# Linear attention beside dilated attention: W2 = KV Wo from 32x32 array tiles, KV^T from 32-column tiles

## The chip, the cores and the metric

The kernel runs on one core of a Trainium2 chip. The time is the device time of one launch in microseconds. Before the change it is 491.19 us, the median of three runs (490.68 to 491.39); the profiled execution has a span of 489.7 us.

## The reference: two attention blocks on one input, mixed by a gate

```python
# x: 2048 x 1024 bf16; 32 heads of 32
g = sigmoid((x * gate_w).sum(-1, keepdims=True))
out = g * A(x) + (1 - g) * B(x)

def A(x):                                   # linear attention
    q, k, v = split_heads(x @ wqkv_A)
    phi = lambda t: where(t > 0, t + 1, exp(t)) + 1e-6
    pq, pk = phi(q), phi(k)
    kv  = einsum("bhsd,bhse->bhde", pk, v)  # one 32x32 matrix per head
    z   = einsum("bhsd->bhd", pk)
    num = einsum("bhqd,bhde->bhqe", pq, kv)
    den = einsum("bhqd,bhd->bhq", pq, z)[..., None] + 1e-6
    return merge_heads(num / den) @ wo_A

def B(x):                                   # window of 8 keys, 2 apart, softmax
    ...
    return merge_heads(o) @ wo_B
```

## The kernel before

Block A is rearranged. With KV a block-diagonal matrix of 32 blocks of 32x32, one per head, the output is (pq / den) (KV Wo), so the kernel folds KV into Wo once and calls the product W2; W2 overwrites Wo in SBUF. KV itself comes from G = x^T pk, as KV^T = pk^T V = G^T Wv, of which only the diagonal blocks are wanted. The ratio g / (1 - g) = exp(x . gate_w) is folded into the normalised pq, and the evacuation of the last product scales with 1 - g.

The order of stages is: phi(K) of A, G, KV^T, V of B (with the W2 products set between its matmuls), Q of A beside the rest of V, then K and Q of B with the scores and their products with V set between, and last the two output products in one accumulation. TensorE's instructions keep the order in which the code gives them.

The loads at the start are issued in this order, all from SyncE's queue but one:

```python
WkA = [wpool.tile([P, KT, 512], BF16, name="WkA0", tag="wa")]
nc.sync.dma_start_transpose(out=xT[:, :, 0:P], in_=rows(x, 0, P))
for i in range(4):
    if i == 2:
        nc.sync.dma_start_transpose(out=xT[:, :, P:2 * P], in_=rows(x, P, 2 * P))
    (nc.sync if i else nc.scalar).dma_start(            # the first quarter: ScalarE's queue
        out=WkA[0][:, 2 * i:2 * i + 2, :], in_=A_wqkv[...])
for t in range(2, NB):                                  # 14 more transposes
    nc.sync.dma_start_transpose(out=xT[:, :, t * P:(t + 1) * P], in_=rows(x, t * P, (t + 1) * P))
WkA += load_w("WkA", A_wqkv, D, "wa", only=(1,))        # the second half of Wk
...
```

TensorE runs 36 small products of ones first, and then phi(K) for row blocks 0 and 1 in the order in which the quarters come: depths 0 to 3 of block 0, depths 0 to 3 of block 1, then 4 and 5 of both, then 6 and 7 of both. KV^T and W2:

```python
for c in range(KT):                    # eight chunks of 128 columns, four heads in each
    kvp = ps_1.tile([P, P], F32, name="kv_ps", tag="p1")
    for kt in range(KT):
        nc.tensor.matmul(kvp[:], lhsT=WvA[c // 4][:, kt, (c % 4) * P:(c % 4 + 1) * P],
                         rhs=G[c // 4][:, kt, (c % 4) * P:(c % 4 + 1) * P],
                         start=(kt == 0), stop=(kt == KT - 1))
    nc.vector.tensor_tensor(out=KVT[:, c, :], in0=kvp[:], in1=bdmask[:], op=ALU.mult)
...
def w2_event(c):
    def go():
        for half in range(2):
            w2p = bank1()              # one of six banks of ps_1
            nc.tensor.matmul(w2p[:], lhsT=KVT[:, c, :], rhs=WoA[half][:, c, :], start=True, stop=True)
            if half:
                nc.scalar.copy(out=WoA[half][:, c, :], in_=w2p[:])
            else:
                nc.vector.tensor_copy(out=WoA[half][:, c, :], in_=w2p[:])
    return go
...
units = [u for t in range(4) for u in v_units(t)]      # 64 V matmuls of B, groups of 8
interleave(units, [(4 + 8 * c, w2_event(c)) for c in range(KT)])
for t in range(12):
    for u in v_units(4 + t): u()
    for u in qa_units(t, bank1, qa_finish): u()
```

bdmask is 1 in the four 32x32 blocks of the diagonal and 0 elsewhere. Each Q group of A goes through phi, and each row block through the normalising, on VectorE:

```python
def phi(dst, pj):
    e = work.tile([P, 512], F32, name="e", tag="e")
    nc.scalar.activation(out=e[:], in_=pj[:], func=ACT.Exp)
    nc.vector.tensor_scalar(out=e[:], in0=e[:], scalar1=1.0, scalar2=1e-6, op0=ALU.min, op1=ALU.add)
    nc.vector.scalar_tensor_tensor(out=dst, in0=pj[:], scalar=0.0, in1=e[:], op0=ALU.max, op1=ALU.add)

def normalize(t, pq, pn, prod):
    nc.vector.tensor_tensor(out=prod, in0=pq, in1=zrow[:], op=ALU.mult)          # L274
    den = small3.tile([P, H], F32, name="den", tag="den")
    nc.vector.tensor_reduce(out=den[:], in_=prod.rearrange("p (h e) -> p h e", h=H), ...)
    nc.vector.tensor_scalar(out=den[:], in0=den[:], scalar1=1e-6, ...)           # L278
    nc.vector.reciprocal(out=den[:], in_=den[:])
    nc.vector.scalar_tensor_tensor(                                              # L280
        out=pn.rearrange("p (h e) -> p h e", h=H), in0=pq.rearrange("p (h e) -> p h e", h=H),
        scalar=ratio[:, t:t + 1], in1=den[:]..., op0=ALU.mult, op1=ALU.mult)
```

For row blocks 0 to 11 the result is written to DRAM and read back transposed; for the last four it is transposed from SBUF.

Of the kernel before, what the change touches and what calls it, by code (L numbers as in the profile page):

```python
# [9 lines left out]
ALU = mybir.AluOpType  # L10
BF16 = mybir.dt.bfloat16
F32 = mybir.dt.float32
PE = mybir.EngineType.PE
DVE = mybir.EngineType.DVE
P = 128
# [14 lines left out]
def interleave(units, events):  # L30

    events = sorted(events, key=lambda e: e[0])
    for i, unit in enumerate(units):
        while events and events[0][0] <= i:
            events.pop(0)[1]()
        unit()
    for _, fn in events:
        fn()
# [3 lines left out]
def kernel(  # L42
# [11 lines left out]
    nc = tc.nc  # L54
    S, D = A_x.shape[1:]
# [3 lines left out]
    out2 = out[0].rearrange("(m two) d -> two m d", two=2)  # L59

    def rows(ap, s0, s1):
        return ap[s0 // 1024, s0 % 1024:(s1 - 1) % 1024 + 1, :]

    H = 32
    Dh = D // H
    KT = D // P
    NB = S // P
# [4 lines left out]
    consts = ctx.enter_context(tc.tile_pool(name="consts", bufs=1))  # L72
    wpool = ctx.enter_context(tc.tile_pool(name="wpool", bufs=2))
# [5 lines left out]
    def load_w(name, src, col0, tag, only=(0, 1)):  # L79
        halves = []  # L80
        for h in only:
            w = wpool.tile([P, KT, 512], BF16, name=f"{name}{h}", tag=tag)
            c0 = col0 + h * 512
            nc.sync.dma_start(out=w[:], in_=src[:, c0:c0 + 512].rearrange("(kt p) n -> p kt n", p=P))
            halves.append(w)
        return halves
# [7 lines left out]
    WkA = [wpool.tile([P, KT, 512], BF16, name="WkA0", tag="wa")]  # L94
    nc.sync.dma_start_transpose(out=xT[:, :, 0:P], in_=rows(x, 0, P))  # L95
    for i in range(4):
        if i == 2:
            nc.sync.dma_start_transpose(out=xT[:, :, P:2 * P], in_=rows(x, P, 2 * P))
        (nc.sync if i else nc.scalar).dma_start(  # L99
            out=WkA[0][:, 2 * i:2 * i + 2, :],  # L100
            in_=A_wqkv[2 * i * P:(2 * i + 2) * P, D:D + 512].rearrange("(kt p) n -> p kt n", p=P))
    for t in range(2, NB):
        nc.sync.dma_start_transpose(out=xT[:, :, t * P:(t + 1) * P], in_=rows(x, t * P, (t + 1) * P))  # L103
    WkA += load_w("WkA", A_wqkv, D, "wa", only=(1,))
# [3 lines left out]
    WvA = load_w("WvA", A_wqkv, 2 * D, "wb")  # L108
    WoA = load_w("WoA", A_wo, 0, "wo")
# [3 lines left out]

    onesb = consts.tile([P, P], BF16, name="onesb")
    nc.vector.memset(onesb[:], 1.0)
    bdmask = consts.tile([P, P], F32, name="bdmask")
    nc.vector.memset(bdmask[:], 0.0)
    for i in range(4):
        nc.vector.memset(bdmask[32 * i:32 * i + 32, 32 * i:32 * i + 32], 1.0)


    def band(dst, lead):
# [11 lines left out]
    ratio = consts.tile([P, NB], F32, name="ratio")  # L134
    omg = consts.tile([P, NB], F32, name="omg")
    zrow = consts.tile([P, D], F32, name="zrow")
    KVT = consts.tile([P, KT, P], BF16, name="KVT")

    work = ctx.enter_context(tc.tile_pool(name="work", bufs=3))
    small3 = ctx.enter_context(tc.tile_pool(name="small3", bufs=2))  # L140
# [7 lines left out]
    with tc.manual_schedule(engines={PE}):  # L148

        with ExitStack() as s1:  # L150
            ps_1 = s1.enter_context(tc.tile_pool(name="ps_1", bufs=6, space=bass.MemoryType.PSUM))
# [37 lines left out]
            for t in range(1, NB):  # L189
                side.append(lambda t=t: nc.vector.tensor_tensor(  # L190
                    out=zacc[:], in0=zacc[:] if t > 1 else pk[:, 0, :], in1=pk[:, t, :], op=ALU.add))
            side.append(lambda: nc.gpsimd.partition_all_reduce(zrow[:], zacc[:], P, bass_isa.ReduceOp.add))
            for t in range(NB):
                side.append(lambda t=t: nc.vector.tensor_tensor_reduce(
                    out=gjunk[:], in0=xrow[:, t, :], in1=gw_row[:], scale=1.0, scalar=0.0, op0=ALU.mult,
                    op1=ALU.add, accum_out=gdot[:, t:t + 1]))

            G = []
            for half in range(2):
                g_ = kq.tile([P, KT, 512], BF16, name=f"G{half}", tag="kq")  # L200
                G.append(g_)
                for kt in range(KT):
                    pj = ps_1.tile([P, 512], F32, name="g_ps", tag="p1")
                    for t in range(NB):
                        nc.tensor.matmul(pj[:], lhsT=xrow[:, t, kt * P:(kt + 1) * P],  # L205
                                         rhs=pk[:, t, half * 512:(half + 1) * 512],
                                         start=(t == 0), stop=(t == NB - 1))
# [7 lines left out]
            nc.vector.tensor_scalar(out=omg[:], in0=ratio[:], scalar1=1.0, scalar2=None, op0=ALU.add)  # L215
            nc.vector.reciprocal(out=omg[:], in_=omg[:])

            for c in range(KT):
                kvp = ps_1.tile([P, P], F32, name="kv_ps", tag="p1")
                for kt in range(KT):  # L220
                    nc.tensor.matmul(kvp[:], lhsT=WvA[c // 4][:, kt, (c % 4) * P:(c % 4 + 1) * P],  # L221
                                     rhs=G[c // 4][:, kt, (c % 4) * P:(c % 4 + 1) * P],
                                     start=(kt == 0), stop=(kt == KT - 1))
                nc.vector.tensor_tensor(out=KVT[:, c, :], in0=kvp[:], in1=bdmask[:], op=ALU.mult)
            WkB = load_w("WkB", B_wqkv, D, "wb")


# [9 lines left out]
            def bank1():  # L237
                return ps_1.tile([P, 512], F32, name="p1_ps", tag="p1")

            def w2_event(c):  # L240
                def go():
                    for half in range(2):
                        w2p = bank1()
                        nc.tensor.matmul(w2p[:], lhsT=KVT[:, c, :], rhs=WoA[half][:, c, :], start=True, stop=True)  # L244
                        if half:
                            nc.scalar.copy(out=WoA[half][:, c, :], in_=w2p[:])
                        else:
                            nc.vector.tensor_copy(out=WoA[half][:, c, :], in_=w2p[:])
                return go

            def v_units(t):
# [21 lines left out]
# [3 lines that stand above are left out]
                nc.vector.tensor_reduce(out=den[:], in_=prod.rearrange("p (h e) -> p h e", h=H),  # L276
                                        axis=mybir.AxisListType.X, op=ALU.add)
                nc.vector.tensor_scalar(out=den[:], in0=den[:], scalar1=1e-6, scalar2=None, op0=ALU.add)  # L278
                nc.vector.reciprocal(out=den[:], in_=den[:])
                nc.vector.scalar_tensor_tensor(  # L280
                    out=pn.rearrange("p (h e) -> p h e", h=H), in0=pq.rearrange("p (h e) -> p h e", h=H),
                    scalar=ratio[:, t:t + 1], in1=den[:].rearrange("p (h o) -> p h o", o=1).broadcast_to([P, H, Dh]),
                    op0=ALU.mult, op1=ALU.mult)

            def qa_units(t, bank, evacuate):
                def mm(half, kt, st):
# [16 lines left out]
                    nc.sync.dma_start(out=pqd[t * P:(t + 1) * P, :], in_=pn)  # L303

            units = [u for t in range(4) for u in v_units(t)]
            interleave(units, [(4 + 8 * c, w2_event(c)) for c in range(KT)])
            for t in range(12):
                for u in v_units(4 + t):
                    u()
# [5 lines left out]
        with ExitStack() as s2:  # L315
# [102 lines left out]
            WoB = load_w("WoB", B_wo, 0, "wb")  # L418
            raw = wpool.tile([P, 4, D], BF16, name="raw", tag="wc")
            fw = wpool.tile([P, 2, D], F32, name="fw", tag="wc")  # L420
            pqT = [kq.tile([P, KT, 512], BF16, name="pqT0", tag="kq")]
            for t in range(4):
                nc.sync.dma_start_transpose(out=pqT[0][:, :, t * P:(t + 1) * P], in_=pqd[t * P:(t + 1) * P, :])
# [4 lines left out]
            def qa_late(t):  # L428
                r = raw[:, t - 12, :]
                for half in range(2):  # L430
                    h = slice(half * 512, (half + 1) * 512)
                    phi(r[:, h], r[:, h])
                normalize(t, r, r, fw[:, t % 2, :])
                nc.sync.dma_start_transpose(out=pqT[1][:, :, (t - 4) * P:(t - 3) * P], in_=r)

            def out_units(tb, bank):
                def mm(c0, n, side, c, st):
                    if side == 0 and c == 0:
                        st["ps"] = bank()
                    if side == 0:  # L440
                        lhsT, W = (pqT[0][:, c, tb * P:(tb + 1) * P] if tb < 4 else
                                   pqT[1][:, c, (tb - 4) * P:(tb - 3) * P]), WoA
                    else:
                        lhsT, W = OBT[:, c, tb * P:(tb + 1) * P], WoB
                    nc.tensor.matmul(st["ps"][:, 0:n], lhsT=lhsT, rhs=W[c0 // 512][:, c, c0 % 512:c0 % 512 + n],  # L445
                                     start=(side == 0 and c == 0), stop=(side == 1 and c == KT - 1))
                    if side == 0 or c < KT - 1:
                        return
                    osb = work.tile([P, 512], BF16, name="osb", tag="e")
                    nc.scalar.activation(out=osb[:, 0:n], in_=st["ps"][:, 0:n], func=ACT.Copy,  # L450
                                         scale=omg[:, tb:tb + 1])
                    (nc.sync if tb < NB - 1 else nc.scalar).dma_start(
                        out=rows(out2, tb * P, (tb + 1) * P)[:, c0:c0 + n], in_=osb[:, 0:n])
                parts = [(0, 512), (512, 512)] if tb < NB - 1 else [(0, 512), (512, 256), (768, 256)]
                for c0, n in parts:
                    st = {}
                    for side in range(2):
                        for c in range(KT):
                            yield lambda c0=c0, n=n, side=side, c=c, st=st: mm(c0, n, side, c, st)
# [51 lines left out]
```

The softmax here doesn't subtract the row's maximum and nothing guards it: scores larger than these inputs give would overflow.

## Time and profile before

| | us |
|---|---|
| median of three runs | 491.19 |
| span of the profiled execution | 489.7 |
| TensorE matmuls busy | 483.1 |
| VectorE busy | 279.1 |
| ScalarE busy | 188.0 |
| phi(K), second half of the columns, from | 35.21 |
| G from | 63.01 |
| KV^T from | 118.26 |
| V of B with W2 in between from | 121.8 |
| V of B and Q of A in turn from | 142.56 |
| K and Q of B with scores from | 221.98 |
| last stage (outputs) from | 382.75 |

A line of the profile names the source line, the engine (PE is TensorE, PEld its weight load, DVE VectorE, ACT ScalarE, SPq the queue of SyncE), the operation, and the tiles written and read. In the timeline and in the chain the first number is the start and the second the length, in microseconds; x16 is the number of instructions merged into the line; what stands in brackets is the engine's idle time before it and what ended it. [...] matmuls that follow each other every 0.22 us are shown as 0.38 us long; the rate is read from the starts.

### The profile page before, as it was taken

To read this page: it belongs to the slowest core of one execution; us is meant where nothing else is said; L and a number is where in the kernel's file an instruction comes from. 1 tells how busy PE (TensorE), PEld (TensorE's weight loads), DVE (VectorE), ACT (ScalarE), POOL (GpSimd) and SP (SyncE) were. 2 spreads that over 40 slices of the span, in tenths; PEclk is the share of its full clock that TensorE was granted. 3 is DMA by queue.
4 is the path that set the end of the run, shared out by engine and by line. 5 is a ranking of instruction groups with operands and counts; after the bars stand their busy time and mean duration, and the time that the engine had idled before them with its cause. 6 is when DMAs were issued, how large, how long until landed. Compare 5 with 4: busy or idle time off the path is not lost.

```text
span 489.7 us, 8140 instructions
## 1 busy us (share of the span) xinstructions
PE 483.1 (99%) x3332; PEld 229.5 (47%) x3332; DVE 279.1 (57%) x512; ACT 188.0 (38%) x283; POOL 16.3 (3%) x33
## 2 busy tenths in 40 slices
PE   7999999999999999999999999999999999999997
PEld 4444444446444444444454444445444444444444
DVE  1666689993329999996356666556655596000000
ACT  1333311111543333333566666666664332212121
POOL 3100001411000000000000000000000000000000
PEclk9999999999999999999999999999999999999999
DMA  9999960000521222245011151111173943111111
GB/s 195 165 289 370 348 201 0 0 1 28 194 73 59 82 95 93 72 135 174 3 38 28 32 115 30 30 36 35 31 151 82 213 87 86 33 43 33 43 34 43
DMA packets 80181, 46.56 MB, mean 95 GB/s; under 512 B 53520, under 2 KB 74128, under 8 KB 80144
## 3 DMA queue, kind: packets, MB, share of 16 engines
q1 hardware_dynamic: 79440, 45.52, 35.1%
q8 instruction: 26, 0.43, 0.4%
q10 hardware_dynamic: 704, 0.52, 0.4%
q14 instruction: 11, 0.09, 0.1%
HBM read 21.23 MB, written 7.34 MB: 58 GB/s over the span
## 4 chain that ended last, share of the span: by engine, by line
PE 92%; SPq 5%; DMA 2%; issue 0%; ACT 0%
PE kq_ps L332 23%; PE d_ps L445 21%; PE g_ps L205 11%; PE p_ps L255 11%; PE p_ps L289 8%; PE pk_ps L157 6%; SPq L103 4%; PE q_ps L289 3%; PE oB L383 3%; PE s L358 2%; DMA WkA<-in_A_wqkv_dram 2%; PE q_ps L445 1%; PE kv_ps L221 1%; PE p_ps L244 1%; SPq L99 0%; SPq L95 0%
## 5 line engine op out<-in xcount | busy, mean ns | idle before, releaser
L368 ACT ACTIVATE PT<-s 128x896 bf16<-128x896 f32 (+1 forms) x72 | 63.0, 926 | 24.5 <-PE s L358 24.5
L332 PE MATMUL kq_ps<-xT,WkB 128*128 128x512 bf16 x256 | 65.3, 379 | 0.0
L332 PE MATMUL kq_ps<-xT,WqB 128*128 128x512 bf16 x256 | 64.8, 379 | 0.0
L369 DVE TENSOR_TENSOR PT<-PT,mask 128x896 bf16<-128x896 bf16 (+1 forms) x72 | 44.6, 623 | 26.6 <-ACT PT L368 26.6
L255 PE MATMUL p_ps<-WvB,xT 128*128 128x512 bf16 x256 | 58.5, 379 | 0.0
L157 PE MATMUL pk_ps<-WkA,xT 128*128 128x512 bf16 x256 | 56.2, 379 | 2.2 <-DMA WkA<-in_A_wqkv_dram 1.6
L445 PE MATMUL d_ps<-WoA,pqT 128*128 128x512 bf16 (+1 forms) x248 | 56.9, 372 | 0.0
L445 PE MATMUL d_ps<-WoB,OBT 128*128 128x512 bf16 (+1 forms) x248 | 56.9, 372 | 0.0
L205 PE MATMUL g_ps<-pk,xrow 128*128 128x512 bf16 x256 | 55.4, 379 | 0.0
L145 DVE TENSOR_SCALAR e<-e 128x512 f32<-128x512 f32 x64 | 27.4, 428 | 42.3 <-ACT e L144 42.3
L450 ACT ACTIVATE osb<-d_ps,omg 128x512 bf16<-128x512 f32 (+1 forms) x31 | 20.9, 673 | 76.1 <-PE d_ps L445 73.3
L289 PE MATMUL p_ps<-WqA,xT 128*128 128x512 bf16 x192 | 43.4, 379 | 0.0
L337 ACT CAST kqt<-kq_ps 128x512 bf16<-128x512 f32 x48 | 28.2, 587 | 31.8 <-PE kq_ps L332 31.6
L157 PEld LDWEIGHTS <-xT 128*128 128x128 bf16 x256 | 24.6, 98 | 33.3 <-DMA xT<-in_A_x_dram 2.0
L445 PEld LDWEIGHTS <-pqT 128*128 128x128 bf16 x264 | 25.8, 98 | 29.5
L445 PEld LDWEIGHTS <-OBT 128*128 128x128 bf16 x264 | 25.8, 98 | 29.3
L205 PEld LDWEIGHTS <-xrow 128*128 128x128 bf16 x256 | 25.0, 98 | 30.2
L255 PEld LDWEIGHTS <-xT 128*128 128x128 bf16 x256 | 25.0, 98 | 30.0
L289 PEld LDWEIGHTS <-xT 128*128 128x128 bf16 x256 | 24.3, 98 | 28.5
L144 ACT ACTIVATE e<-pk_ps 128x512 f32<-128x512 f32 x32 | 19.0, 597 | 42.6 <-PE pk_ps L157 42.6
L332 PEld LDWEIGHTS <-WqB 128*128 128x128 bf16 x256 | 23.0, 97 | 24.7
L332 PEld LDWEIGHTS <-WkB 128*128 128x128 bf16 x256 | 22.6, 97 | 24.1
(57 smaller groups left out, 399.7 us busy)
## 6 DMA issues: line engine op xcount, KB each, us to landing
xrow<-in_A_x_dram SPq DMA_DIRECT2D x4, 1024.0 KB, 13.0
out_dram<-osb SPq DMA_DIRECT2D x30, 128.0 KB, 1.9
pqd<-tmp SPq DMA_DIRECT2D x12, 256.0 KB, 2.1
WvA<-in_A_wqkv_dram SPq DMA_DIRECT2D x2, 1024.0 KB, 16.0
WoA<-in_A_wo_dram SPq DMA_DIRECT2D x2, 1024.0 KB, 12.2
WvB<-in_B_wqkv_dram SPq DMA_DIRECT2D x2, 1024.0 KB, 11.9
WqA<-in_A_wqkv_dram SPq DMA_DIRECT2D x2, 1024.0 KB, 9.6
WkB<-in_B_wqkv_dram SPq DMA_DIRECT2D x2, 1024.0 KB, 6.4
```

What stands on the lines that cost most here:

```text
L103: nc.sync.dma_start_transpose(out=xT[:, :, t * P:(t + 1) * P], in_=rows(x, t * P, (t + 1) * P))
L145: nc.vector.tensor_scalar(out=e[:], in0=e[:], scalar1=1.0, scalar2=1e-6, op0=ALU.min, op1=ALU.add)
L157: nc.tensor.matmul(pj[:], lhsT=xT[:, kt, t * P:(t + 1) * P], rhs=WkA[half][:, kt, :], start=(kt == 0), stop=(kt == KT - 1))
L205: nc.tensor.matmul(pj[:], lhsT=xrow[:, t, kt * P:(kt + 1) * P], rhs=pk[:, t, half * 512:(half + 1) * 512], start=(t == 0), stop=(t == NB - 1))
L255: nc.tensor.matmul(st["pj"][:], lhsT=xT[:, kt, t * P:(t + 1) * P], rhs=WvB[half][:, kt, :], start=(kt == 0), stop=(kt == KT - 1))
L289: nc.tensor.matmul(st["pj"][:], lhsT=xT[:, kt, t * P:(t + 1) * P], rhs=WqA[half][:, kt, :], start=(kt == 0), stop=(kt == KT - 1))
L332: nc.tensor.matmul(st["pj"][:], lhsT=W[c // 4][:, kt, (c % 4) * P:(c % 4 + 1) * P], rhs=xT[:, kt, cols], start=(kt == 0), stop=(kt == KT - 1))
L337: (nc.vector.tensor_copy if 0 <= after < 4 else nc.scalar.copy)(out=kqt[:, which, cols], in_=st["pj"][:])
L368: nc.scalar.activation(out=ptv[:, hs], in_=s4[:, hs, 0:W_], func=ACT.Exp, scale=SCALE)
L369: nc.vector.tensor_tensor(out=ptv[:, hs], in0=ptv[:, hs], in1=m[:, None, :].broadcast_to([P, 2, W_]), op=ALU.mult)
L445: nc.tensor.matmul(st["ps"][:, 0:n], lhsT=lhsT, rhs=W[c0 // 512][:, c, c0 % 512:c0 % 512 + n], start=(side == 0 and c == 0), stop=(side == ...
L450: nc.scalar.activation(out=osb[:, 0:n], in_=st["ps"][:, 0:n], func=ACT.Copy, scale=omg[:, tb:tb + 1])
```

## The change

KV^T is computed as four tiles of 32 columns, each 128 rows deep, so that only the diagonal blocks are computed: four small matmuls (32 columns in, 32 columns of array) in place of one of 128x128. The mask is no longer needed, and KVT keeps 32 columns for each chunk. W2 is computed with 32x32 tiles of the array: sixteen heads a pass, each with its own 32 rows and 32 columns, into four banks. Tile (r, j) writes bank r and quadrant j, so that head r of chunk 4g + j lands in chunk 4g + r at place j: within a group of four chunks, chunk and place of the heads are exchanged. So the normalised pq must be written in the same exchanged order, which makes one instruction of the normalising three. The last four row blocks can then no longer be normalised in place and get a tile of their own (lw).

Apart from that, the first weight quarter and the three transfers of the last row block of the output go from ScalarE's queue to SyncE's.

```diff
@@ loads at the start
-        (nc.sync if i else nc.scalar).dma_start(
-            out=WkA[0][:, 2 * i:2 * i + 2, :],
-            in_=A_wqkv[2 * i * P:(2 * i + 2) * P, D:D + 512].rearrange("(kt p) n -> p kt n", p=P))
+        nc.sync.dma_start(out=WkA[0][:, 2 * i:2 * i + 2, :],
+                          in_=A_wqkv[2 * i * P:(2 * i + 2) * P, D:D + 512].rearrange("(kt p) n -> p kt n", p=P))
@@ bdmask and its five memsets are taken out
-    KVT = consts.tile([P, KT, P], BF16, name="KVT")
+    KVT = consts.tile([P, KT, 32], BF16, name="KVT")
@@ KV^T
-            for c in range(KT):
-                kvp = ps_1.tile([P, P], F32, name="kv_ps", tag="p1")
-                for kt in range(KT):
-                    nc.tensor.matmul(kvp[:], lhsT=WvA[c // 4][:, kt, (c % 4) * P:(c % 4 + 1) * P],
-                                     rhs=G[c // 4][:, kt, (c % 4) * P:(c % 4 + 1) * P],
-                                     start=(kt == 0), stop=(kt == KT - 1))
-                nc.vector.tensor_tensor(out=KVT[:, c, :], in0=kvp[:], in1=bdmask[:], op=ALU.mult)
+            for g in range(2):
+                kvp = ps_1.tile([P, 4, 32], F32, name="kv_ps", tag="p1")
+                for c in range(4):
+                    for kt in range(KT):
+                        for j in range(4):
+                            cols = slice(c * P + 32 * j, c * P + 32 * j + 32)
+                            nc.tensor.matmul(kvp[32 * j:32 * j + 32, c, :], lhsT=WvA[g][:, kt, cols],
+                                             rhs=G[g][:, kt, cols], start=(kt == 0), stop=(kt == KT - 1))
+                nc.vector.tensor_copy(out=KVT[:, 4 * g:4 * g + 4, :], in_=kvp[:])
@@ W2
-            def w2_event(c):
+            def w2_event(g, half):
                 def go():
-                    for half in range(2):
-                        w2p = bank1()
-                        nc.tensor.matmul(w2p[:], lhsT=KVT[:, c, :], rhs=WoA[half][:, c, :], start=True, stop=True)
-                        if half:
-                            nc.scalar.copy(out=WoA[half][:, c, :], in_=w2p[:])
-                        else:
-                            nc.vector.tensor_copy(out=WoA[half][:, c, :], in_=w2p[:])
+                    w2p = [bank1() for _ in range(4)]
+                    for j in range(4):
+                        for r in range(4):
+                            rs = slice(32 * r, 32 * r + 32)
+                            nc.tensor.matmul(w2p[r][32 * j:32 * j + 32, :],
+                                             lhsT=KVT[rs, 4 * g + j, 0:32],
+                                             rhs=WoA[half][rs, 4 * g + j, :], start=True, stop=True)
+                    for r in range(4):
+                        (nc.scalar.copy if r % 2 else nc.vector.tensor_copy)(
+                            out=WoA[half][:, 4 * g + r, :], in_=w2p[r][:])
                 return go
@@ normalize
-                nc.vector.scalar_tensor_tensor(
-                    out=pn.rearrange("p (h e) -> p h e", h=H), in0=pq.rearrange("p (h e) -> p h e", h=H),
-                    scalar=ratio[:, t:t + 1], in1=den[:].rearrange("p (h o) -> p h o", o=1).broadcast_to([P, H, Dh]),
-                    op0=ALU.mult, op1=ALU.mult)
+                nc.vector.tensor_scalar(out=den[:], in0=den[:], scalar1=ratio[:, t:t + 1], scalar2=None, op0=ALU.mult)
+                for g in range(2):
+                    nc.vector.tensor_tensor(
+                        out=pn[:, 512 * g:512 * g + 512].rearrange("p (r j e) -> p j r e", r=4, j=4),
+                        in0=pq[:, 512 * g:512 * g + 512].rearrange("p (j r e) -> p j r e", r=4, j=4),
+                        in1=den[:, 16 * g:16 * g + 16].rearrange("p (j r o) -> p j r o", r=4, o=1)
+                        .broadcast_to([P, 4, 4, Dh]), op=ALU.mult)
@@ where W2 stands among the 64 V matmuls
-            interleave(units, [(4 + 8 * c, w2_event(c)) for c in range(KT)])
+            interleave(units, [(8 + 12 * (2 * g + half), w2_event(g, half)) for g in range(2) for half in range(2)])
@@ last four row blocks
+            lw = wpool.tile([P, 4, D], BF16, name="lw", tag="wa")
...
-                normalize(t, r, r, fw[:, t % 2, :])
-                nc.sync.dma_start_transpose(out=pqT[1][:, :, (t - 4) * P:(t - 3) * P], in_=r)
+                pn = lw[:, t - 12, :]
+                normalize(t, r, pn, fw[:, t % 2, :])
+                nc.sync.dma_start_transpose(out=pqT[1][:, :, (t - 4) * P:(t - 3) * P], in_=pn)
@@ output transfers
-                    (nc.sync if tb < NB - 1 else nc.scalar).dma_start(
-                        out=rows(out2, tb * P, (tb + 1) * P)[:, c0:c0 + n], in_=osb[:, 0:n])
+                    nc.sync.dma_start(out=rows(out2, tb * P, (tb + 1) * P)[:, c0:c0 + n], in_=osb[:, 0:n])
```

## The prediction

> **What bounds the kernel now.** I read the page's utilisation first, then the chain that ended last, then the groups and the timelines of the four stages the change touches.
>
> ```profile
> PE 483.1 (99%) x3332; PEld 229.5 (47%) x3332; DVE 279.1 (57%) x512; ACT 188.0 (38%) x283; POOL 16.3 (3%) x33
> ...
> PEclk9999999999999999999999999999999999999999
> ```
>
> TensorE is occupied all the time at the full granted clock, the other engines are not. The chain agrees, apart from the start:
>
> ```profile
> 27.05 8.11 DMA WkA<-in_A_wqkv_dram
> 35.21 27.80 PE pk_ps L157 x128
> 63.01 55.25 PE g_ps L205 x256
> 118.26 3.57 PE kv_ps L221 x64
> 123.13 1.73 PE p_ps L255 x8
> 125.29 1.73 PE p_ps L255 x8
> ```
>
> From 35.2 us to the last evacuation the chain is TensorE in its own order. So after that point only two things move the end: TensorE time itself, or a new stall of TensorE. Two spacings follow. KV^T: 64 matmuls in 3.57 us, 55.8 ns each. A 512-column matmul: 1.73 / 8 = 0.216 us, or 0.42 ns a column; and between 123.13 + 1.73 = 124.86 and 125.29 lie 0.43 us for the two W2 matmuls, again 0.216 each. All W2 costs 16 x 0.216 = 3.45 us. KV^T and W2 together are 7.0 us, 1.4% of the kernel: the change cannot gain more.
>
> Before 35.2 us the chain is SyncE issuing transfers one after another. Timeline of the start:
>
> ```profile
> 0.80 1.34 SPq L95 DMA_TRANSPOSE xT<-in_A_x_dram  x1
> 0.83 0.44 ACTq L99 DMA_DIRECT2D WkA<-in_A_wqkv_dram  x1
> ...
> 2.20 0.56 SPq L99 DMA_DIRECT2D WkA<-in_A_wqkv_dram  x1
> 2.82 1.25 SPq L98 DMA_TRANSPOSE xT<-in_A_x_dram  x1
> ...
> 6.13 0.59 PE L157 MATMUL pk_ps<-WkA,xT 128*128 128x512 bf16 x2 [0.87 <-DMA WkA<-in_A_wqkv_dram]
> ```
>
> The first weight quarter is issued by ScalarE at 0.83 us, beside SyncE's first transpose; the next quarter is SyncE's at 2.20 and TensorE gets it at 6.13, 3.9 us later.
>
> **VectorE in the V/Q stage (142 to 222 us).** One row block of V and one of Q take TensorE 32 x 0.216 = 6.91 us. VectorE is the only engine that comes near that, and the change adds to it there:
>
> ```profile
> 161.68 1.23 DVE L274 TENSOR_TENSOR tmp<-tmp,zrow 128x1024 f32<-128x1024 bf16 x1
> ...
> 164.19 0.18 DVE L278 TENSOR_SCALAR den<-den 128x32 f32<-128x32 f32 x1
> 164.41 0.35 DVE L279 RECIPROCAL den<-den 128x32 f32<-128x32 f32 x1
> 164.79 1.28 DVE L280 SCALAR_TENSOR_TENSOR tmp<-tmp,ratio,den 128x1024 bf16<-128x1024 bf16 x1
> 166.00 0.42 DVE L145 TENSOR_SCALAR e<-e 128x512 f32<-128x512 f32 x1
> ...
> 167.40 0.43 DVE L145 TENSOR_SCALAR e<-e 128x512 f32<-128x512 f32 x1 [0.25 <-ACT e L144]
> ```
>
> Its only pause in a period is 0.25 us, the wait for ScalarE's exp of the second half. It is used 6.91 - 0.25 = 6.66 us of 6.91.
>
> **What the trace already shows of tiles.** The scores of block B are 32-row tiles:
>
> ```profile
> 235.63 0.81 PE L332 MATMUL kq_ps<-xT,WkB 128*128 128x512 bf16 x3
> ...
> 236.38 0.38 PE L358 MATMUL s<-kqt 32*128 32x128 bf16 x16
> 236.69 1.25 PE L332 MATMUL kq_ps<-xT,WkB 128*128 128x512 bf16 x5
> 241.00 0.56 PE L383 MATMUL oB<-V,PT 128*128 128x33 bf16 x16
> ```
>
> The third kq matmul starts at 235.63 + 2 x 0.216 = 236.06; the first score should follow at 236.28 and comes at 236.38: 0.10 us for the way in. Sixteen scores occupy 0.31 us up to the next kq matmul. Four tiles at a time, each streams 128 + 3 x 112 = 464 columns, 0.20 us; so 0.11 us for the way back. Their individual records show four different row tiles starting 3 to 5 ns apart. The oB matmuls (33 columns, full array) come 25 ns apart (16 in 0.40 us, to the next matmul at 241.40).
>
> [...]
>
> **The change part by part.**
>
> W2. Out: 3.45 us. In: four passes of 16 tiles, each pass one stream of 512 columns (0.216) plus 15 starts of 4 ns (0.06) plus both ways of the mode change (0.2): an estimate of 0.48 us, four of them 1.9. Saving 1.5 us. A pass takes four of the six banks. The two VectorE copies take 2 x 0.69 = 1.4 us and the two ScalarE copies 2 x 0.59 = 1.2 us; the next pass comes 12 V matmuls later, 2.6 us. The third pass reuses the bank of the third V group, which ends 8 V matmuls (1.7 us) earlier, so I expect no stall.
>
> KV^T. Out: 3.57 us. In: 256 matmuls of 32 columns, 64 rounds of four column tiles. If the tiles work side by side, a round is the 25 ns that a small matmul with its load took in oB, plus three starts of 4 ns: 64 x 37 ns = 2.4 us, with the mode change 2.6. Saving 1.0 us. This is the least certain step. Eight masked copies of 0.29 us become two copies, off the path.
>
> Normalising. The 1.28 us instruction becomes a scale of den (0.18 plus a gap, 0.22 a slot, like L278) and two products of 512 elements. From L274 [...] each is 0.69 us. Slots: 0.22 + 0.73 + 0.66 = 1.61 against 166.00 - 164.79 = 1.21 now, so 0.40 us more in each period. VectorE then needs 6.66 + 0.40 = 7.06 of 6.91 us and falls behind by 0.15 us a period, some 2 us by the twelfth. A Q bank is now free 2.1 us after its group (165.0 to 167.1) and is wanted again only after five more groups, 8.6 us. TensorE should not notice. The lag ends before VectorE's next duty, the copy at 230.65: it now finishes at 228.2.
>
> The start. The first quarter goes behind the 1.34 us transpose on SyncE: issued at 2.20 instead of 0.83, and everything behind it 0.6 us later. TensorE begins at about 6 instead of 4.65, reaches its steady stream (8.53 now) 0.5 us later, and the second half of WkA (issued 27.05, landed 35.16) is also up to 0.6 later. TensorE waits only 0.52 us for that now, so nothing absorbs it unless the transfers and not the issues set the landing. I take +0.5 us.
>
> The tail. The last transfers are issued from SyncE: both queues start within 0.03 us of the evacuation that they wait for (486.43 + 0.47, issue 486.93 on ScalarE; 479.53 + 0.69, issue 480.24 on SyncE). Zero.
>
> Sum: -1.5 - 1.0 + 0.5 = -2.0, from 491.2 to 489.2 us.
>
> **The rivals.** (1) Column tiles do not overlap, [...]. Then each of the 256 pairs costs the 25 ns of oB: 6.4 us, 2.8 more than now, and W2, if its column tiles are serial too, 4 x (4 x 0.216 + 0.2) = 4.3 us, 0.8 more. The kernel ends at 492.7 to 494.8. [...] (2) Load and matmul do not even overlap each other [...] Against: loads run ahead everywhere in this trace. (3) VectorE becomes the bound of the V/Q stage. For it: 7.06 over 6.91. It would need a lag of 6.5 us to reach TensorE, 0.8 us a period rather than 0.40; strided writes twice as slow would do that, and cost up to 3 us. (4) The first quarter's move is hidden altogether: 488.7.
>
> **Range and chances.** My weights: 60% that column tiles overlap, 30% rival 1, 10% rival 2 or a mixture. The first alone gives 489 plus or minus 0.7; leaning towards the others I say 489.5. The range must hold rival 1 in its milder form: 488.2 to 493.5. Two per cent is 9.8 us: 7.0 us at stake cannot make that gain, and only rival 2 with everything else against it makes that loss.
>
> **What would show it.** Right: KV^T's chain piece falls to 2 to 3 us, the gaps between V groups that hold a W2 pass are near 0.48 us (four of them), L280's successors fill the 0.25 us pause, the first 512-column stream without a break begins near 9.0 us, and WkA's second half lands near 35.7. Wrong: KV^T at 6 us or more, TensorE waiting for VectorE in front of a W2 pass or a Q group, or a W2 pass near 1 us.

## The result, and the profile after

| | median, us | runs | ratio to before, 95% interval |
|---|---|---|---|
| before | 490.98 | 6 | |
| the change | 493.29 (492.33 to 494.38) | 6 | 1.0045 (1.0028 to 1.0062) |

The change costs 2.3 us, or 0.45%. The profiled execution, the fastest of the six, took 492.33 us with a span of 490.6 us; that of the kernel before took 491.39 us with a span of 489.7. The page of the changed kernel, busy times and granted clock:

```profile
PE 481.4 (98%) x3572; PEld 226.9 (46%) x3572; DVE 280.4 (57%) x533; ACT 187.5 (38%) x283; POOL 15.9 (3%) x33
...
PEclk9999999999899999999999999999999999999999
```

TensorE is busy 1.7 us less than before and the kernel is longer: TensorE now stands still somewhere, and in the eleventh slice its clock is not full. The chain that ended last, its pieces around KV^T:

```profile
62.85 55.25 PE g_ps L200 x256
119.74 2.20 issue
122.64 2.93 PE p_ps L258 x8
126.16 2.95 PE p_ps L258 x12
129.47 2.70 PE p_ps L258 x12
132.53 2.70 PE p_ps L258 x12
```

G begins at 62.85 us (63.01 before), so the start costs nothing here. Then there are 2.20 us of "issue", in which TensorE waits for nothing that the profile shows. The first eight V matmuls take 2.93 us instead of 1.73; later twelve take 2.70 us, 0.22 each, again. Between such groups a W2 pass leaves 0.36 us (126.16 + 2.95 = 129.11 to 129.47). The timeline of the same stretch:

```profile
118.03 1.71 PE L220 MATMUL kv_ps<-G,WvA 128*32 128x32 bf16 x187
...
121.95 0.70 PE L220 MATMUL kv_ps<-G,WvA 128*32 128x32 bf16 x69 [2.20 <-issue]
...
122.58 3.00 PE L258 MATMUL p_ps<-WvB,xT 128*128 128x512 bf16 x8
```

The pause lies in the middle of the 256 small matmuls, after 187 of them. The clock of that stretch, by windows (the columns are the window, its length, the busy time and instructions of each engine, the granted clock, the DMA engines' share, GB/s):

```profile
119.80:121.90 2.10, 0.00 (x0) 0.00 (x0) 0.00 (x0) 0.00 (x0) 0.00 (x0) 1.00 0.64 191
122.60:123.50 0.90, 0.90 (x10) 0.43 (x5) 0.29 (x1) 0.00 (x0) 0.00 (x0) 0.85 1.06 368
123.50:126.10 2.60, 2.60 (x22) 0.61 (x20) 0.00 (x0) 0.49 (x1) 0.00 (x0) 0.50 0.87 280
126.60:127.50 0.90, 0.90 (x6) 0.40 (x5) 0.90 (x2) 0.76 (x2) 0.00 (x0) 0.98 0.58 198
```

The compute engines are all idle in the pause. From 123.23 us, 1.3 us after the end of the pause, the clock is halved, and full again at 126.64 us.

The account of the profiled executions, by the starts in their chains. From the end of G to the first V matmul: 118.26 to 121.83 before, 118.10 to 122.64 after, so 1.0 us longer; without the 2.2 us of pause it would be 1.2 shorter. From there to the stage in which V and Q alternate: 121.83 to 142.56 before, 122.64 to 143.47 after, 0.1 us longer. In it 80 V matmuls take 17.27 us and the W2 matmuls took 3.45; four passes at 0.47 (0.36 and what the change of tile mode takes from the V piece, 2.70 - 2.59) take 1.9, so 20.83 - 17.27 - 1.9 = 1.7 us are lost to the low clock. From there to the end: 347.1 us in both. Sum: -0.2 at the start, -1.2 and +2.2, -1.6 and +1.7: +0.9, the difference of the spans.

The other runs of the changed kernel lie up to 2 us higher. The 3.41 us at half clock lower the mean over 490.6 us to 0.997; twice as long would lower it to 0.993, and three of the six runs have 0.993. They have no trace, so where their clock was low is not shown.

### The profile page after: what moved, and what is told of

It is laid out like the page before. It is cut to its first block, busy times and chain, and to the rows that moved or that the text cites. A ratio compares the mean times of both kernels' runs of the same rounds, so it can differ in the third digit from the quotient of the medians.

```text
span 490.6 us, 8646 instructions
## 1 busy us (share of the span) xinstructions
PE 481.4 (98%) x3572; PEld 226.9 (46%) x3572; DVE 280.4 (57%) x533; ACT 187.5 (38%) x283; POOL 15.9 (3%) x33
## 4 chain that ended last, share of the span: by engine, by line
PE 97%; DMA 1%; issue 1%; SPq 0%; ACT 0%; ACTq 0%
PE kq_ps L339 23%; PE d_ps L454 21%; PE p_ps L258 12%; PE g_ps L200 11%; PE pk_ps L152 11%; PE p_ps L296 8%; PE q_ps L296 3%; PE oB L390 3%; PE s L365 2%; PE q_ps L454 1%; DMA xT<-in_A_x_dram 1%; PE kv_ps L220 0%; PE p_ps L246 0%; SPq L95 0%; SPq L99 0%
## 5 line engine op out<-in xcount | busy, mean ns | idle before, releaser
L263 ACT CAST tmp<-p_ps 128x512 bf16<-128x512 f32 x32 | 18.8, 589 | 39.6 <-PE p_ps L258 39.6
```

## The experiments

**Theory: TensorE runs out of instructions.** The page counts 26 transfers of instructions on queue 8 before, 28 after; TensorE executes 6,664 and 7,144 matmuls and weight loads. Either way that is one transfer for some 256 of them. The lines of the two pages, before and after:

```profile
q8 instruction: 26, 0.43, 0.4%
...
q8 instruction: 28, 0.46, 0.4%
```

256 of them, 128 matmuls with their loads, last 28 us at 0.216 us a pair, but 1.1 us at the 8.3 ns a pair of the column tiles. The theory is my inference from these counts: the instructions are used up faster than they arrive. The trace names nothing that TensorE waits for; it shows one such transfer at 119.33 us and TensorE going on at 121.95. Then the pause drops the clock.

Rivals: (1) WkB's two 1 MB loads, issued at 119.31 us, hold up the fetch. (2) The lightly used array, not the pause, drops the clock. (3) The pause is the tiles' own, for instance at the change of bank between the two groups.

**Moving WkB's load.**

```diff
 # e1_wkb_later
-            WkB = load_w("WkB", B_wqkv, D, "wb")
...
             interleave(units, [(8 + 12 * (2 * g + half), w2_event(g, half)) ...])
+            WkB = load_w("WkB", B_wqkv, D, "wb")
```

> Only the two 1 MB loads of WkB move: they are issued after the first 64 V matmuls instead of right after KV^T, so no large transfer runs during KV^T. Theory (TensorE's 512 instructions of KV^T, 4.2 ns apart, run out of fetched instructions: [...]): the pause stays, 1.9 to 2.4 us after some 180 to 250 small matmuls, and the time stays that of the changed kernel, 492 to 494.5 us. Rival 1 (WkB's transfer, issued at 119.31 us, holds up the instruction fetch): the pause falls under 0.7 us, the clock does not drop, 488.5 to 489.8 us.

493.47 us, 1.0052 (1.0037 to 1.0067). It tells nothing of rival 1: the order in the code does not fix when SyncE issues, and the loads still went out at 119.81 us. It is the changed kernel once more: a pause of 1.95 us after 187 matmuls. So the load got a dependency:

```diff
 # e9_wkb_gated, behind the W2 copies on VectorE
+            for h in range(2):
+                wk = wpool.tile([P, KT, 512], BF16, name=f"WkB{h}", tag="wb")
+                nc.vector.memset(wk[:, 0, 0:1], 0.0)
+                nc.sync.dma_start(out=wk[:], in_=B_wqkv[...])
```

> The trial of rival 1 again, since in e1_wkb_later the transfers were still issued during KV^T (at 119.81 us): now each of WkB's tiles gets one element written by VectorE behind the W2 copies, and the loads wait for that. Theory (instructions run out by themselves): the fetch is not disturbed, so it may be a little quicker, but the pause stays, 1.6 to 2.3 us, and so does the lower clock after it; 491.5 to 494 us. Rival 1 (WkB's transfer holds up the fetch): under 0.7 us of pause, 488.5 to 490 us.

491.66 us, 1.0013 (1.0003 to 1.0024). The transfers of e9_wkb_gated from 117 to 124 us (the first row gives the DMA share of 40 slices in tenths), and its timeline:

```profile
DMA  0000000000004000000000000000000004000000
...
DMA packets 2, 0.03 MB, mean 5 GB/s; under 512 B 0, under 2 KB 0, under 8 KB 0
...
q8 instruction: 2, 0.03, 2.4%
```

```profile
117.59 1.71 PE L220 MATMUL kv_ps<-G,WvA 128*32 128x32 bf16 x187
...
121.72 0.73 PE L220 MATMUL kv_ps<-G,WvA 128*32 128x32 bf16 x69 [2.42 <-issue]
...
122.38 3.27 PE L258 MATMUL p_ps<-WvB,xT 128*128 128x512 bf16 x8
```

In these 7 us nothing moves but two transfers of instructions, the first at 119.1 us (slice 13 of 0.175 us), and TensorE stands still just the same, 2.42 us, until 2.6 us after that transfer began. Rival 1 falls. In the profiled run the eight V matmuls right behind the pause are slow: 3.27 us, where 1.90 is usual. Ten of the 20 runs, this one among them, have a mean clock of 0.997 or 0.993 (491.8 us and more); in the rest the mean stayed at 1.0, 490.2 to 491.5 us. In the changed kernel all six are at 0.997 or lower.

**Doubling the burst.**

```diff
 # e5_kv_twice
-                for c in range(4):
+                for c in [c for c in range(4) for _ in range(2)]:
```

> The changed kernel with each chunk of KV^T computed twice (512 small matmuls, the second time over the first; the result is the same): a burst of 1024 instructions. Theory [...]: the pauses multiply, three in all, some 128 matmuls apart from the second on, each 1.9 to 2.5 us; KV^T from first to last 10.5 to 12 us against 4.5. Rival 3 (one pause at the change of groups or of banks): one pause, KV^T 6.5 to 7 us.

Its timeline:

```profile
117.81 1.69 PE L220 MATMUL kv_ps<-G,WvA 128*32 128x32 bf16 x187
...
121.64 1.22 PE L220 MATMUL kv_ps<-G,WvA 128*32 128x32 bf16 x128 [2.15 <-issue]
...
125.65 1.23 PE L220 MATMUL kv_ps<-G,WvA 128*32 128x32 bf16 x128 [2.79 <-issue]
...
129.65 0.73 PE L220 MATMUL kv_ps<-G,WvA 128*32 128x32 bf16 x69 [2.78 <-issue]
...
130.32 3.57 PE L258 MATMUL p_ps<-WvB,xT 128*128 128x512 bf16 x8
```

Three pauses, and each of the two stretches between them has 128 matmuls with their 128 loads, as many instructions as the page counts to one transfer. Rival 3 in its form of one pause at the group change falls. The stretches begin 4.0 us apart (121.64, 125.65, 129.65), so KV^T takes 12.5 us instead of at most 12: from the first pause on TensorE gets through one instruction in 15.6 ns. The single run took 500.16 us.

**Slowing the consumption.**

```diff
 # e4_kv_wide: stream 128 columns, then copy the diagonal blocks out
-                kvp = ps_1.tile([P, 4, 32], F32, name="kv_ps", tag="p1")
+                kvp = ps_1.tile([P, 4, P], F32, name="kv_ps", tag="p1")
...
-                                             rhs=G[g][:, kt, cols], ...)
+                                             rhs=G[g][:, kt, c * P:(c + 1) * P], ...)
```

> The changed kernel with the same 256 small matmuls, but each streams 128 columns instead of 32 (the diagonal blocks are then copied out): same instructions, slower consumption, some 14 ns a matmul instead of 8.4. Theory: the pause is the fetch time less the time in which the instructions at hand are used up, so it shrinks by about 128 x 5.6 ns = 0.7 us, to 1.2 to 1.7 us; KV^T with its pause takes 5.0 to 5.6 us against 4.5. Rivals 1 and 3 (a fixed cost of the transfer or of the tiles): the pause stays at 2.1 us or more.

```profile
118.41 2.80 PE L220 MATMUL kv_ps<-G,WvA 128*32 128x128 bf16 x187
...
122.95 1.17 PE L220 MATMUL kv_ps<-G,WvA 128*32 128x128 bf16 x69 [1.74 <-issue]
...
124.05 1.90 PE L260 MATMUL p_ps<-WvB,xT 128*128 128x512 bf16 x8
```

The pause comes after the same 187 matmuls and shrinks to 1.74 us, a little above the 1.2 to 1.7 expected. KV^T with its pause takes 5.6 us, 1.1 more than in the changed kernel, yet the time is 491.24 us, 1.0008 (0.9999 to 1.0018), 2 us less than the changed kernel: the V matmuls behind run at full clock (1.90 us for eight, with the last one's length), and 14 of the 15 runs have a mean clock of 0.999 or 1.0.

**A pause with the full array.** To part the pause from the small tiles, KV^T goes back to full matmuls, and TensorE is made to wait in the middle of it.

```diff
 # e2_kv_full: KV^T by 64 full matmuls, diagonal blocks copied into the compact KVT
+                kvp = ps_1.tile([P, 4, P], F32, name="kv_ps", tag="p1")
+                for c in range(4):
+                    cols = slice(c * P, (c + 1) * P)
+                    for kt in range(KT):
+                        nc.tensor.matmul(kvp[:, c, :], lhsT=WvA[g][:, kt, cols], rhs=G[g][:, kt, cols], ...)
+                for j in range(4):
+                    r = slice(32 * j, 32 * j + 32)
+                    nc.vector.tensor_copy(out=KVT[r, 4 * g:4 * g + 4, :], in_=kvp[r, :, r])
 # e11_full_pause: the same, and ahead of the second group's matmuls
+                if g:
+                    for _ in range(2):
+                        nc.vector.memset(kvp[:], 0.0)
```

> The change with KV^T undone: 64 full 128x128 matmuls as before, of which the four diagonal blocks are copied into the compact KVT; W2 passes, normalising and loads as in the changed kernel. Theory: KV^T 3.6 us, no pause, no clock drop, four W2 passes of 0.47 us each: 1.5 us less than before for W2 and 0.2 less for the start, 489.0 to 489.7 us. Rival 2 (the clock drops because of the small tiles, not because of the pause): the clock drops during or after the W2 passes, over 490.5 us.

489.46 us, 0.9977 (0.9966 to 0.9987), as expected: 1.3 us less than before. Its chain shows each W2 pass as 0.36 or 0.37 us between full-speed V groups.

```profile
118.20 3.57 PE kv_ps L219 x64
121.77 1.73 PE p_ps L259 x8
123.50 0.36 PE p_ps L247 x16
123.86 2.70 PE p_ps L259 x12
```

> e2_kv_full (full 128x128 matmuls, no small tiles in KV^T) with a pause made on purpose: VectorE clears the bank of the second KV^T group twice, behind its copies of the first, and TensorE waits for that, some 2.3 to 2.8 us in the middle of KV^T. Theory A (the pause alone drops the clock): half clock behind the pause in most runs, 493 to 495 us. Theory B (a pause of this length drops it only together with the lightly loaded small-tile phase around it): the mean clock stays at 0.999 or 1.0 in nearly all runs, e2_kv_full's 489.46 plus the pause, 491.5 to 492.3 us.

494.58 us, 1.0073 (1.0047 to 1.0099). The timeline and two windows of e11_full_pause:

```profile
124.10 3.52 PE L222 MATMUL kv_ps<-G,WvA 128*128 128x128 bf16 x32 [2.63 <-DVE kv_ps L218]
...
127.41 1.99 PE L262 MATMUL p_ps<-WvB,xT 128*128 128x512 bf16 x8
```

```profile
124.00:126.00 2.00, 1.90 (x19) 1.94 (x20) 0.00 (x0) 0.00 (x0) 0.00 (x0) 0.54 1.00 344
126.00:128.00 2.00, 2.00 (x19) 1.72 (x17) 0.33 (x2) 0.00 (x0) 0.00 (x0) 0.60 0.00 0
```

Behind a pause of 2.63 us with no small tile near it the clock is low as well: 0.54 and 0.60 in these two windows, 1.00 before 124 and after 128 us. So theory A holds: the pause is enough. The time overstates it: these two windows cost 1.7 us of full clock, while the mean of 0.992 over 493.9 us means some 4 us, so the clock was low elsewhere in this run too; where is not shown. Two of the four runs, the profiled one among them, have a mean clock of 0.992 and take 495.7 us. One has 0.997 (493.49 us), and where its clock was low is not known. The fourth, at 1.0, took 492.14.

The timelines put side by side the pause and the first eight V matmuls behind KV^T, which take 1.89 us, with the last one's length, where there was no pause (e2_kv_full):

| trace | pause (the last one), us | eight V matmuls, us |
|---|---|---|
| e4_kv_wide | 1.74 | 1.90 |
| e1_wkb_later | 1.95 | 3.40 |
| changed kernel | 2.20 | 3.00 |
| e9_wkb_gated | 2.42 | 3.27 |
| e5_kv_twice | 2.78 | 3.57 |

In e11_full_pause the eight take 1.99 us, because there 32 matmuls of KV^T stand between the pause and them; these take 3.52 us, against 1.95 ahead of it. So the matmuls were slow behind each of these pauses but e4's. What decides it is not shown: the pause's length alone does not sort the runs, since all six runs of the changed kernel have a lowered mean but only 10 of 20 of e9, with a longer pause in its trace.

**Keeping the tiles, without the pause.** Two bursts of 256 instructions, one in the middle of G's second half:

```diff
 # e3_kv_split: the loop body over c, kt, j becomes kv_group(g)
                     nc.scalar.copy(out=g_[:, kt, :], in_=pj[:])
                     ...
+                    if half == 1 and kt == 3:
+                        kv_group(0)
...
+            kv_group(1)                     # where KV^T was
 # e8_kv_split_late (and e12): the second burst behind eight V matmuls
-            kv_group(1)
...
-            interleave(units, [(8 + 12 * (2 * g + half), w2_event(g, half)) ...])
+            interleave(units, [(8, lambda: kv_group(1)), (16, w2_event(0, 0)), (28, w2_event(0, 1)),
+                               (40, w2_event(1, 0)), (52, w2_event(1, 1))])
```

> The changed kernel with KV^T's two groups of 128 small matmuls apart: the first stands in the middle of G's second half (its own half of G is ready by then), the second where it was. Each burst is 256 instructions. Theory: no pause in either (or under 0.3 us), no clock drop, each group 1.1 to 1.3 us with the way in and out; 1.0 us less than before for KV^T, 1.5 for W2, 0.2 for the start: 487.9 to 488.8 us. Rival 2 (clock drop from small tiles): no pause, but half clock for some 3 us after a group, 489.5 to 491. Rival 3 (the pause is the tiles' own, for example at the change of banks between the groups): a pause of about 2 us stays.

488.77 us, 0.9965 (0.9953 to 0.9977). No pause like that of the changed kernel; eight of ten runs have a mean clock of 0.999 or 1.0, two 0.997. The second burst waited 0.39 us for ScalarE's copy of the last part of G.

> e3_kv_split with its second KV^T group behind the first eight V matmuls, because it waited 0.4 us for ScalarE's copy of the last part of G; the four W2 passes come 8 V matmuls later. Theory: that wait goes, no pause, no clock drop: 0.4 us less than e3_kv_split (488.77), 488.0 to 488.7, the best of all. Rival [...]: a pause of up to 2 us comes back, 489.5 to 492 us.

488.38 us, 0.9954 (0.9941 to 0.9966). Its timeline:

```profile
104.61 1.20 PE L199 MATMUL kv_ps<-G,WvA 128*32 128x32 bf16 x128
...
105.73 13.99 PE L210 MATMUL g_ps<-pk,xrow 128*128 128x512 bf16 x64
...
121.38 1.20 PE L199 MATMUL kv_ps<-G,WvA 128*32 128x32 bf16 x128
...
122.51 1.90 PE L261 MATMUL p_ps<-WvB,xT 128*128 128x512 bf16 x8
```

The same 256 small matmuls, 1.1 us for each half until the next matmul begins, nothing idle around them. This also speaks against rivals 2 and 3: in the traces of e3 and e8 neither the pause nor slow V matmuls follow the tiles (1.90 us for eight in e8), and the profiled runs of e3, e8, e10 and e12 have a mean clock of 0.999 or 1.0.

**The start.**

```diff
 # e7_before_quarter_sp: the kernel before, with
-        (nc.sync if i else nc.scalar).dma_start(out=WkA[0][:, 2 * i:2 * i + 2, :], in_=...)
+        nc.sync.dma_start(out=WkA[0][:, 2 * i:2 * i + 2, :], in_=...)
 # e10_split_late_act: e8_kv_split_late with that change the other way round
```

> The kernel before with the first weight quarter issued from SyncE, nothing else. As predicted: +0.5 us. What the changed kernel's trace suggests instead: TensorE is 0.6 us behind at 8.3 us, but the wait for the second half of WkA at 35 us (0.5 us) goes, since the transfers and not their issue set its landing: within 0.3 us of before.

490.89 us against 490.78, 1.0009 (0.9999 to 1.0020). TensorE's first products in e7 and the chain behind:

```profile
5.93 0.59 PE L156 MATMUL pk_ps<-WkA,xT 128*128 128x512 bf16 x2 [0.79 <-DMA WkA<-in_A_wqkv_dram]
...
7.76 29.01 PE L156 MATMUL pk_ps<-WkA,xT 128*128 128x512 bf16 x133 [0.48 <-DMA xT<-in_A_x_dram]
```

```profile
7.76 54.69 PE pk_ps L156 x252
62.46 55.25 PE g_ps L204 x256
```

TensorE begins later, but from 7.76 us on phi(K) is one piece without the wait at 35 us that the kernel before has: the second half of WkA was issued 0.2 us later (27.26) and landed 1.8 us earlier (6.1 instead of 8.1 us on the way). Four of the 13 runs of e7 have a mean clock of 0.997 and take 492.3 to 492.8 us. Those four have no trace. In two profiled runs with the same late start phi(K) itself is longer: 57.39 us for 256 matmuls in e1 and 55.40 for 252 in e8, where e7 takes 54.69 for 252; e8's mean clock is 1.0 all the same, so that a mean of 1.0 does not exclude it. Over all runs without a pause in KV^T, 9 of the 45 with the late start (e2, e3, e7, e8, e12) have a mean of 0.997, and 3 of the 82 with the early one (the kernel before, e10). So a lowered mean came more often with the late start, which the medians hide: e7's 13 runs have a mean time of 491.4 us, those of the kernel before beside it 491.0.

> e8_kv_split_late with the first weight quarter on ScalarE's queue, as in the kernel before. Since e7_before_quarter_sp showed 0.1 us for the move, within 0.4 us of e8_kv_split_late, 487.9 to 488.8; if the late start (first product at 5.9 instead of 4.65 us) is what gave 4 of 13 runs of e7 a lower clock, fewer runs with a mean clock of 0.997.

> e8_kv_split_late once more, beside e10 on the same chip: 488.0 to 488.7.

e10: 488.24 us, 0.9949 (0.9937 to 0.9961), all six runs at 0.999 or more. e12: 488.60 us, 0.9960 (0.9946 to 0.9973), two of eight at 0.997. The two medians are not apart by more than their spread. e10 is the best seen: 0.5% below the kernel before, and some 5 us below the change as it was.

## Why the prediction was right and where it was not

The measured 493.29 us lies in the range of 488.2 to 493.5, near its edge, and within 2%. That is luck: the range reached up so far for rival 1, serial column tiles, and the runs show that they are not serial. The point, 489.5, was 3.8 us too low and on the wrong side of before: the loss was not one that I named. Rival 1's own sum was also off: its terms give 493.0 to 495.3, not 492.7 to 494.8.

- **W2.** Right. A pass was put at 0.48 us and takes 0.47, with both ways of the mode change; sixteen tiles side by side, and no wait for a bank. e2_kv_full, which has this part without the small KV^T matmuls, is 1.3 us faster than before.
- **KV^T, the matmuls.** Right, and slightly better than estimated: column tiles do overlap. A round of four was put at 37 ns and takes 33 (8.3 ns a matmul in the individual records); KV^T without its pause is 2.3 us where 2.6 were predicted. Rival 1 of the prediction, which put a pair at 25 ns, falls, and so does rival 2, in which a load and a matmul do not overlap, and whose size no trace had shown: the 8.3 ns hold both a load and a matmul of 32 columns, which at 0.42 ns a column would last 13.5 ns by itself.
- **KV^T, the step that failed.** "In: 256 matmuls of 32 columns, 64 rounds of four column tiles" took the instructions to be at hand. Half of it could be seen: the page before counts 26 transfers of instructions, one for some 256, and at some 9 ns a pair 256 instructions are gone in 1.2 us. That 256 take 4.0 us with the pause was seen only in e5. The gap costs 2.2 us (shown by e5, e9 and e4) and the low clock behind it 1.7 us in the profiled run (shown by e11 to come from such a pause). These 3.9 us outweigh the saving of 2.8.
- **Normalising.** The mechanism was right, the size too large: 0.28 us more in a period instead of 0.40. The scale of den takes a slot of 0.28, and the two products of 512 elements together 1.21 (165.99 to 167.20), no more than the one instruction did. VectorE's timeline in the changed kernel:

```profile
165.71 0.24 DVE L284 TENSOR_SCALAR den<-den,ratio 128x32 f32<-128x32 f32 x1
165.99 1.29 DVE L286 TENSOR_TENSOR tmp<-tmp,den 128x512 bf16<-128x512 bf16 x2
167.20 0.42 DVE L140 TENSOR_SCALAR e<-e 128x512 f32<-128x512 f32 x1
167.65 0.69 DVE L141 SCALAR_TENSOR_TENSOR tmp<-p_ps,e 128x512 bf16<-128x512 f32 x1
168.31 0.43 DVE L140 TENSOR_SCALAR e<-e 128x512 f32<-128x512 f32 x1
```

  The pause ahead of the second e is filled, as predicted, and the period stays 6.90 us (167.20, next at 174.10). Rival 3, VectorE as the bound, did not come.
- **The start.** Put at +0.5 us, measured as +0.1 by the medians; the interval (-0.1 to +1.0 us) does not exclude 0.5, but the traces show where it goes: in the changed kernel the second half of WkA was issued 0.4 us later (27.43) and landed at 34.0 us, not 35.7. The step "nothing absorbs it unless the transfers and not the issues set the landing" took the wrong branch: the landing did not follow the issue. What the move does cost, a lower mean clock in some runs, was not foreseen.
- **The tail.** Zero, as predicted: the last 347.1 us are the same.

## What to carry to other kernels

Packing small matmuls into array tiles multiplies the instructions and shortens each: 256 matmuls with their loads at 8.3 ns a pair came with a pause of 2.2 us here. So count instructions and not only array time, and part a long burst by long matmuls. Bursts of 256 instructions with some 14 us of full matmuls between them did not stop here (e3_kv_split), one of 512 stopped after 374; lengths between, and closer bursts, were not tried. A gap of 2.2 us on TensorE cost nearly twice its length here, because 1.7 us more were lost at half clock behind it. And what a change saves should be looked for in the trace part by part, even where the total says that it lost: here both ideas were good, and the order of the instructions lost more than they won.

## What the runs showed of the hardware that was not expected

- In a burst of 1,024 instructions of small column tiles (e5_kv_twice) TensorE stopped three times, for 2.15, 2.79 and 2.78 us. The stretches between began 4.0 us apart with 256 instructions each, 15.6 ns an instruction.
- Four 128x32 column tiles run side by side: 8.3 ns a matmul with its load in the changed kernel, for 32 columns streamed, where 32 columns at 0.42 ns would take 13.5. With 128 columns streamed 187 take 2.80 us, against 1.71, with the last one's length in both (e4_kv_wide).
- The granted clock was half for 3.41 us in the changed kernel, from 1.3 us after the end of its pause of 2.20 us. In e11_full_pause it was 0.54 in the first 2 us from the end of a pause of 2.63 us. Behind the 1.74 us of e4_kv_wide the matmuls kept their speed.
